# First MLP weight in 14 column-pair places, refilled with resident units one by one; row transfers of the third group issued from GpSimd

## The chip, the core and the metric

The kernel runs on one core of one Trainium2 chip. The core has five engines that work side by side, each with a queue of its own that it takes in order: TensorE (PE; its weight loads are listed apart as PEld), VectorE (DVE), ScalarE (ACT), GpSimd (POOL) and SyncE (SP). SP here does nothing but issue DMA transfers; ACT and POOL issue some as well. All transfers share the core's 16 DMA engines. The metric is device time in microseconds from one execution of the whole program, lower being better; the median of three runs stands for a kernel.

## The reference: what is computed

Two branches are added to the input x (2048 rows of 1024, bfloat16), both of them fed with the normalised rows xn.

```python
xn = _layernorm(x, axis=-1)
return x + _A_ref(xn, mem0, Wq, Wk, Wv, Wo, seg_len) + _B_ref(xn, w1, b1, w2, b2)

# A: a recurrence over 64 segments of 32 rows, 32 heads of 128, 8 memory rows
for s in range(n_seg):
    h = jnp.concatenate([mem, xs], axis=1)                # 40 rows
    q, k, v = h @ Wq, h @ Wk, h @ Wv                      # each 1024 x 4096
    p = _softmax(jnp.where(mask, q k^T * scale, -1e9))
    o = (p v) @ Wo                                        # 4096 x 1024
    mem = o[:, :M, :].copy()
    outs.append(o[:, M:, :])

# B: an MLP
h = _gelu(jnp.einsum('bsd,df->bsf', x, w1) + b1)          # w1 1024 x 3584
return jnp.einsum('bsf,fd->bsd', h, w2) + b2              # w2 3584 x 1024
```

The lines of A are shortened into matrix products. Because a segment's memory is the output of the segment before it, the 64 segments must be done one after another. The four attention weights hold 33.5 MB together[...].

## The kernel before, in words

**The MLP stage.** The rows are handled in four groups (tg 0 to 3) of four tiles of 128 rows. For each group, xn transposed lies in two places (xn0 and xn1 for even groups, xn2 and xn3 for odd ones). The first matrix product (L506) makes 28 column blocks of 128, each of them eight matmuls over the depth of 1024 (kt), then GELU on ACT and DVE writes to gT0 to gT6. The second product (L555, in the last group L591) reads gT and the second weight in 14 places w2_0 to w2_13. Its results are written to a DRAM array R_n (keep_R) and from there copied, in pieces of 8 or 32 rows, to two DRAM arrays hr_d and hrL_d in the order in which the recurrence will want them (turn_R, L425 to L454). The input rows of a group lie in pairs in xt0 to xt3; the last group's in xt2 and xt3.

**The first weight.** It lies in 16 places w1_0 to w1_15, one for each kt and half of the columns, of 128 partitions x 1792 columns. Each column block reads eight of these places, so none is free before its half is done, and load_w1 fills the first half in two column parts.

**The places.** All these names are places of one size (128 x 2048 bfloat16, 0.524 MB). A *unit* is a piece of an attention weight of that size: 16 each for K, Q and V, 16 for O (two heads of Wo). Of the 64 units, 46 are *resident*: they are fetched once, into places which the MLP has left, and stay. The other 18 are *streamed*: fetched for every segment anew, into six ring places, in the order of use. RING and RES_PLACES (L196 to L201) say which place gets which. start_stream (L240 to L256) fills a ring place with the next streamed unit; most streamed units are read from contiguous copies in DRAM (Wc_K, Wc_Q, Wc_V, Wc_O) that the kernel makes at the end of the first group. Two streamed units are held in PSUM banks and copied from there (L240); one of them is brought in through half_home and d_oL. fetch_resident fills places with resident units, and what has no place left is fetched *late*, during segment step 0 (late_units, fetch_late), one unit for each streamed unit that is done.

**The change of stages.** At the start of the last group SP issues the rows for step 0 (load_x_rows, load_left_rows) and refills xt0 and xt1. After the first product of that group it starts the six ring places, loads half_home and the other w1 places; during the second product it refills w2 and gT places as they fall free; after it, xt2 and xt3, which must wait until keep_R has written their contents to R_n.

**The recurrence.** Each of the 64 steps runs K, Q, V (two halves of eight units each, products L705 of four 32-row column tiles) and O (16 units, L902). Between them come transposes, scores, column sums (L834, L840), the exponentials (ACT L845, L848), weights (DVE L855, L859) and values (L874, L880). Step 0 makes, for all six halves, a second product with the rows left over from the 24 main ones (hrL); in the others one or two halves do. After each unit, unit_done refills its ring place, then takes one entry of late_units, then one or two of `small`, a list of small transfers that POOL issues.

**The order.** There is no scheduler: each engine's queue holds the instructions in the order of the program text, and SP's queue is where all weight transfers stand. An SP instruction whose place isn't free holds up all behind it.

Of the kernel before, what the change touches and what calls it, by code (L numbers as in the profile page):

```python
# [17 lines left out]
P = 128  # L18
# [5 lines left out]
F = 3584  # L24
# [3 lines left out]
KT = DM // P  # L28
FC = F // P
# [57 lines left out]
def kernel(  # L87
# [63 lines left out]
    def slab(place):  # L151
        if place in low:
            return low[place]
        return slabs.tile([P, 2048], BF16, name="u", tag=place)
# [38 lines left out]

    RING = [f"xn{k}" for k in range(4)] + [f"w1_{k}" for k in range(16)]  # L196
    RES_PLACES = list(low) + ["xt0", "xt1"] + RING[STREAM_BUFS:]
    RING = RING[:STREAM_BUFS]
    for k in range(7):
        RES_PLACES += [f"w2_{2 * k}", f"w2_{2 * k + 1}", f"gT{k}"]  # L200
    RES_PLACES += ["xt2", "xt3"]  # L201
    UNIT_AT = dict(zip(RES_PLACES, RESIDENT))
    res_tiles = {}


# [17 lines left out]
    def fetch_resident(*places):  # L223
        for place in places:
            unit = UNIT_AT[place]
            res_tiles[unit] = slab(place)[:, :]
            fetch(res_tiles[unit], unit)
# [14 lines left out]
    def start_stream(slot):  # L242
        if not starts:
            return
        n = starts.popleft()
        unit, t = streams[n], slab(slot)
        if unit in kept_in:
            for c0, bank in kept_in[unit]:
                copy_bits(t[:, c0:c0 + 1024].bitcast(U32), bank.bitcast(U32))
        elif unit == PART:  # L250
            nc.sync.dma_start(out=t[:, PART_COLS:], in_=copies[unit])
        elif unit in copies:
            nc.sync.dma_start(out=t[:, :], in_=copies[unit])
        else:
            fetch(t[:, :], unit)
        stream_tiles[n], slot_of[n] = t, slot  # L256
# [8 lines left out]
    def load_left_rows(g, eng=nc.sync):  # L265
        hr = hrp.tile([P, 256], BF16, name="hrL")
        eng.dma_start(out=hr[:, :], in_=hrL_d[g, :, 0:256])
        nxt["hL"] = hr.rearrange("p (k t) -> p k t", k=KT)
# [27 lines left out]
    with tc.tile_pool(name="ma", bufs=2) as ma, tc.tile_pool(name="mps", bufs=6, space=PSUM) as mps:  # L296
# [17 lines left out]
        nc.vector.memset(o_sb[:, 0:8, :], 0.0)  # L314
        w1_sb, w2_sb = [], []

        def load_w1(half):
            for kt in range(KT):
                w1_sb.append(slab(f"w1_{8 * half + kt}")[:, 0:F // 2])
            for c in (0, 1) if half == 0 else (None,):  # L320
                for kt in range(KT):
                    cs = slice(0, F // 2) if c is None else slice(F // 4 * c, F // 4 * c + F // 4)
                    nc.sync.dma_start(
                        out=w1_sb[8 * half + kt][:, cs], in_=w1_v[:, kt, F // 2 * half:F // 2 * (half + 1)][:, cs]
                    )
                if c == 0:
                    nc.sync.dma_start(out=b1rows[:, :], in_=B_b1.rearrange("(fc p) -> fc p", p=P))

        b1rows = ma.tile([FC, P], BF16, name="b1rows", bufs=1)
        load_w1(0)  # L330
        masks_out()
        for j in range(4):
            nc.sync.dma_start(
# [2 lines left out]
            )  # L336
        b2row = ma.tile([1, DM], BF16, name="b2row", bufs=1)
        nc.sync.dma_start(out=b2row[:, :], in_=B_b2.rearrange("(o d) -> o d", o=1))
        load_w1(1)
        for i in range(14):  # L340
            t = slab(f"w2_{i}")[:, :].rearrange("p (c d) -> p c d", d=DM)
            nc.sync.dma_start(out=t, in_=w2_v[:, 2 * i:2 * i + 2, :])
# [79 lines left out]

            return seg % GRP == 1 or seg == NSEG - 1

        def turn_R(ttg, small=None):  # L425

            for i in range(4):
                seg = 4 * ttg + i  # L430
                rows = R_n[seg * SEG:(seg + 1) * SEG, :].rearrange("t (j c) -> t j c", j=4)
                og, slot = divmod(seg + 2, GRP)
                both = [
                    t[:, 256:512].rearrange("(h r) c -> r h c", h=2)
                    for t in (hr_d[min(4 * og + 1, NSEG - 1) + 1, :, :], hrL_d[og, :, :])
                ]
                halves = [rows.rearrange("t (h w) c -> t w h c", w=2)[:, w, :, :] for w in range(2)]
                if with_left(seg):
                    m0 = main_row(slot)
                    pairs = [(both[w][m0:m0 + SEG, :, :], halves[w]) for w in range(2)]  # L440
                else:
                    pairs = [(hr_d[seg + 1, :, 256:512].rearrange("(j t) c -> t j c", j=4), rows)]
                rows_at = [NL * slot]
                if seg < 2:
                    rows_at.append(NL * (slot ^ 2))
                elif seg >= NSEG - 2:
                    rows_at.append(main_row(1) + SEG + NL * slot)
                for r0 in rows_at:
                    pairs += [(both[w][r0:r0 + NL, :, :], halves[w][NX:SEG, :, :]) for w in range(2)]
                for o, r in pairs:  # L450
                    if small is None:
                        nc.sync.dma_start(out=o, in_=r)
                    else:
                        small.append(lambda o=o, r=r: nc.gpsimd.dma_start(out=o, in_=r))  # L454

# [32 lines left out]
        for tg in range(4):  # L488
            last = tg == 3
            if last:  # L490

                load_x_rows(0)
                load_left_rows(0)
                fetch_resident("xt0", "xt1")
            gts = [slab(f"gT{i}")[:, :].rearrange("p (c t) -> p c t", c=4) for i in range(7)]

            def gelu_tail(fb, u, xb):
                sg = ma.tile([P, 512], BF16, name="g_sg")
                nc.scalar.activation(out=sg[:, :], in_=u[:, :], func=ACT.Sigmoid, scale=GELU_C)
                nc.vector.tensor_tensor(out=gts[fb // 4][:, fb % 4, :], in0=sg[:, :], in1=xb[:, :], op=ALU.mult)  # L500

            pend = None
            for fb in range(FC):
                ps = mps.tile([P, 512], F32, name="ps")
                for kt in range(KT):
                    nc.tensor.matmul(  # L506
                        ps[:, :].rearrange("p (s t) -> p s t", t=SEG),
                        lhsT=w1_sb[fb // 14 * 8 + kt][:, (fb % 14) * P:(fb % 14 + 1) * P],
                        rhs=xnT[kt // 4][:, :, kt % 4, :],
                        start=(kt == 0),  # L510
                        stop=(kt == KT - 1),
                    )
                xb = ma.tile([P, 512], BF16, name="g_xb", bufs=3)
                nc.scalar.activation(  # L514
                    out=xb[:, :], in_=ps[:, :], func=ACT.Identity, bias=b1col[:, fb:fb + 1], scale=1.0
                )
                u = ma.tile([P, 512], BF16, name="g_u")
                nc.vector.tensor_tensor(out=u[:, :], in0=xb[:, :], in1=xb[:, :], op=ALU.mult)
                nc.vector.tensor_scalar(
                    out=u[:, :], in0=u[:, :], scalar1=0.044715, scalar2=1.0, op0=ALU.mult, op1=ALU.add  # L520
                )
                nc.vector.tensor_tensor(out=u[:, :], in0=u[:, :], in1=xb[:, :], op=ALU.mult)  # L522
                if pend is not None:
                    gelu_tail(*pend)
                pend = (fb, u, xb)
            gelu_tail(*pend)

            if tg == 0:
# [6 lines left out]
            if not last:  # L535
# [3 lines left out]
                if tg == 0:  # L539
                    for unit, c in copies.items():  # L540
                        fetch(c, unit)
                    fetch_resident(*low)
                for t in range(4):
                    ln_stats(4 * tg + 4 + t, xtoks[4 * tg + 4 + t])
                ln_sqrt(4 * tg + 4, 4 * tg + 8)
# [20 lines left out]
                    keep_R(ttg, rsb)  # L566
                keep_xT(tg + 1, xnT)
                for t in range(4):
                    turn_R(4 * tg + t)
            else:  # L570


                for slot in RING:
                    start_stream(slot)
                h = 4 * IN_BANKS[1] + 2 * IN_BANKS[2]
                nc.sync.dma_start(out=half_home[:, :], in_=Wo_v[:, h, :])
                fetch_resident(*(place for place in RES_PLACES if place.startswith("w1_")))
                put_mem(o_sb, nxt["hT"], mps.tile([P, 512], F32, name="ps"))
                nc.sync.dma_start(out=d_oL[:, :], in_=Wo_v[:, h + 1, :])
                pss = [mps.tile([P, 512], F32, name="ps") for _ in range(6)]  # L580
# [24 lines left out]
                    cp(out=xtoks[4 * tg + n // 2][:, cs], in_=pss[n][:, :])  # L605
                for t in range(4):
                    keep_R(4 * tg + t, xtoks[4 * tg + t])
                fetch_resident("xt2", "xt3")

# [3 lines left out]
    with tc.tile_pool(name="late", bufs=1) as late, \  # L615
# [42 lines left out]
        def fetch_late(unit):  # L658
            t = late.tile([P, 2048], BF16, name="W_" + "_".join(map(str, unit)))[:, :]
            res_tiles[unit] = t  # L660
            fetch(t, unit)

        late_units = deque(RESIDENT[len(RES_PLACES):])

        def unit_done(unit):

            if IS_STREAMED[unit]:
                start_stream(slot_of.pop(used - 1))
                if late_units:
                    fetch_late(late_units.popleft())  # L670
                for _ in range(2 if len(small) > 8 else 1):
                    if small:
                        small.popleft()()
# [7 lines left out]
        for s in range(NSEG):  # L681
            g, i4 = divmod(s, GRP)
            first, final = s == 0, s + 1 == NSEG
            if 1 <= s <= 4:
                turn_R(NT - 5 + s, small)

# [401 lines left out]
```

The softmax here doesn't subtract the row's maximum and nothing guards it: scores larger than these inputs give would overflow.

## Time and profile before

| | |
|---|---|
| runs of the kernel before | 1868.1, 1876.3, 1877.6 us; median 1876.3 us |
| the profiled execution | span 1866.2 us, from its first to its last instruction; the page gives no other time for it, so what lies around the span is known only as the 1.9 to 11.4 us by which the three runs are longer |
| PE busy | 1726.3 us (93%) |
| DVE, ACT, POOL busy | 904.3 us (48%), 650.4 us (35%), 257.7 us (14%) |
| moved by DMA | 613.13 MB, mean 329 GB/s |
| MLP stage | first matmul of L506 at 16.0 us, last of L591 over by about 422 us |
| recurrence | first product at 423.0 us; end of step 0 (ACT's cast of the memory rows, L1004) at 459.2 us, of step 62 at 1838.9 us |

A line of groups in the profile names the source line, the engine, the operation and the tiles (out<-in). A line of waits reads: engine, tile and line, what it waited for, total us, times, longest us. In the timeline, a line has the start, the length, the engine, the line and the transfer, and how many instructions were merged in it; "SPq" is SP's queue, whose issues are not counted as busy. A wait names what came last.

### The profile page before, as it was taken

The page shows a single profiled execution, that of the slowest core. Times are in us where ns is not written, and L with a number is a line of the kernel's source. Part 1 is how long each engine was busy: PE and PEld are TensorE (multiplying, and loading weights), DVE is VectorE, ACT ScalarE, POOL GpSimd, SP SyncE. Part 2 cuts the span into 40 slices and gives each one's busy share as a digit, 9 for nine tenths or more (in the row PEclk, how much of TensorE's full clock was granted, in tenths as well). Part 3 has the DMA queues.
Part 4 walks back from the last instruction along what each step waited for, and adds up shares of the span by engine and source line. Part 5 has one row for each costly group of instructions (what it writes and reads, how often), then busy time and mean ns, then how long its engine had stood idle before and what let it go on. Part 6 is the DMA issues. An engine that isn't in the chain of part 4 may idle for free.

```text
span 1866.2 us, 72871 instructions
## 1 busy us (share of the span) xinstructions
PE 1726.3 (93%) x32208; PEld 938.2 (50%) x32228; DVE 904.3 (48%) x2190; ACT 650.4 (35%) x1384; POOL 257.7 (14%) x511
## 2 busy tenths in 40 slices
PE   7999999998999999988899999999999999999987
PEld 3444444444554555455555555555545454555544
DVE  6657483704444444444444444544444454544443
ACT  6434251602333333333333333333333333333333
POOL 0000000000442111111111211111111111111112
PEclk9999999999999999999999999999999999999999
DMA  9821211399999999999999999999999999999998
GB/s 337 268 57 47 53 45 53 127 364 334 400 382 393 384 397 379 367 364 368 368 377 380 378 392 394 399 390 384 382 384 390 387 381 378 389 402 384 395 372 318
DMA packets 219721, 613.13 MB, mean 329 GB/s; under 512 B 46507, under 2 KB 65755, under 8 KB 219404
## 3 DMA queue, kind: packets, MB, share of 16 engines
q1 hardware_dynamic: 199292, 589.38, 83.1%
q0 software_dynamic: 15872, 16.39, 2.7%
q8 instruction: 252, 4.13, 0.9%
q10 hardware_dynamic: 4240, 2.71, 0.5%
q14 instruction: 65, 0.53, 0.1%
HBM read 594.40 MB, written 29.23 MB: 334 GB/s over the span
## 4 chain that ended last, share of the span: by engine, by line
PE 65%; DMA 21%; DVE 5%; issue 4%; ACT 3%; POOL 1%; DVEq 0%; ACTq 0%; POOLq 0%; SPq 0%
PE acc L705 30%; PE ps L506 10%; DMA u<-Wc_K 10%; PE acc L902 9%; PE ps L555 8%; DMA u<-Wc_O 4%; DMA outL_d<-half_home 2%; DMA u<-Wc_Q 2%; PE ps L591 2%; ACT mixed L848 2%; PE acc L874 2%; DVE b_oL L763 1%; PE mixed L807 1%; DVE pd_main L855 1%; ACT mixed L845 1%
## 5 line engine op out<-in xcount | busy, mean ns | idle before, releaser
L705 PE MATMUL acc<-u,hr_home 128*32 128x512 bf16 x11520 | 784.3, 381 | 34.5 <-issue 11.8
L705 PEld LDWEIGHTS <-hr_home 128*32 128x32 bf16 x12288 | 353.4, 97 | 318.1 <-issue 64.5
L705 PE MATMUL acc<-u,hrL 128*32 128x512 bf16 x2880 | 261.7, 381 | 9.4 <-issue 5.7
L902 PE MATMUL acc<-u,d_oL 128*32 128x256 bf16 (+1 forms) x3552 | 179.7, 291 | 20.5 <-DMA u<-Wc_O 12.4
L506 PE MATMUL ps<-u 128*128 128x512 bf16 x896 | 196.1, 382 | 2.6 <-ACT u L390 2.6
L240 DVE TENSOR_SCALAR u<-kept 128x512 uint32<-128x512 uint32 x254 | 163.5, 686 | 29.2 <-PE acc L902 12.0
L555 PE MATMUL ps<-u 128*128 128x512 bf16 x657 | 146.2, 379 | 0.8
L902 PEld LDWEIGHTS <-b_oL 128*32 128x32 bf16 x3569 | 112.7, 99 | 67.8 <-issue 35.3
L506 PEld LDWEIGHTS <-u 128*128 128x128 bf16 x896 | 88.1, 98 | 109.3 <-issue 4.6
L902 PEld LDWEIGHTS <-d_oL 128*32 128x32 bf16 (+1 forms) x3552 | 104.0, 98 | 73.7 <-issue 32.6
L1052 POOL DMA_DIRECT2D out_dram<-hr_home x188 | 96.6, 515 | 308.8 <-DVE hr_home L1019 296.2
L855 DVE TENSOR_TENSOR pd_main<-half_home,mixed 128x320 bf16<-128x320 bf16 x128 | 62.5, 488 | 157.5 <-ACT mixed L848 155.7
L705 PEld LDWEIGHTS <-hrL 128*32 128x32 bf16 x3072 | 92.0, 96 | 61.6 <-issue 24.9
L763 DVE STREAM_TRANSPOSE b_oL<-b_oL 128x512 bf16<-128x512 bf16 x128 | 90.7, 708 | 62.5 <-ACT b_oL L749 62.5
L902 PE MATMUL acc<-u,b_oL 128*32 128x256 bf16 (+1 forms) x1618 | 107.0, 292 | 14.9 <-DMA u<-Wc_O 10.5
L902 PE MATMUL acc<-W_O,b_oL 128*32 128x256 bf16 (+1 forms) x1776 | 109.4, 291 | 4.7 <-issue 4.5
L262 POOL DMA_DIRECT2D hr_home<-hr_d x58 | 32.4, 558 | 585.1 <-PE acc L705 566.4
L749 ACT CAST kT<-acc 128x512 bf16<-128x512 f32 x64 | 37.5, 586 | 216.9 <-PE acc L705 216.9
L555 PEld LDWEIGHTS <-u 128*128 128x128 bf16 x672 | 65.3, 98 | 77.4 <-DVE g_u L522 0.4
L749 ACT CAST b_oL<-acc 128x512 bf16<-128x512 f32 x128 | 75.2, 587 | 82.1 <-PE acc L705 81.3
L1004 ACT CAST d_oL<-acc 128x256 bf16<-128x256 f32 (+1 forms) x63 | 26.9, 427 | 209.3 <-PE acc L902 209.3
L514 ACT ACTIVATE g_xb<-ps,b1col 128x512 bf16<-128x512 f32 x112 | 76.8, 686 | 61.0 <-PE ps L506 59.8
(123 smaller groups left out, 1968.3 us busy)
## 6 DMA issues: line engine op xcount, KB each, us to landing
u<-Wc_K SPq DMA_DIRECT2D x320, 512.0 KB
u<-Wc_V SPq DMA_DIRECT2D x256, 512.0 KB
u<-Wc_O SPq DMA_DIRECT2D x256, 512.0 KB
u<-Wc_Q SPq DMA_DIRECT2D x128, 512.0 KB
u<-Wc_O SPq DMA_DIRECT2D x64, 320.0 KB
hr_home<-hr_d POOLq DMA_DIRECT2D x58, 128.0 KB, 5.5
u<-in_B_w_dram SPq DMA_DIRECT2D x14, 512.0 KB
u<-in_A_Wq_dram SPq DMA_DIRECT2D x14, 512.0 KB
```

The lines of the kernel that those rows point to most:

```text
L240: nc.vector.tensor_single_scalar(out=out, in_=in_, scalar=0, op=ALU.bitwise_or)
L506: nc.tensor.matmul(ps[:, :].rearrange("p (s t) -> p s t", t=SEG), lhsT=w1_sb[fb // 14 * 8 + kt][:, (fb % 14) * P:(fb % 14 + 1) * P], rhs=x ...
L514: nc.scalar.activation(out=xb[:, :], in_=ps[:, :], func=ACT.Identity, bias=b1col[:, fb:fb + 1], scale=1.0)
L555: nc.tensor.matmul(ps[:, :], lhsT=gts[fc // 4][:, fc % 4, t * P:(t + 1) * P], rhs=w2_sb[fc // 2][:, fc % 2, cs], start=(fc == 0), stop=(fc ...
L591: nc.tensor.matmul(pss[2 * t + nb][:, :], lhsT=gts[fc // 4][:, fc % 4, t * P:(t + 1) * P], rhs=w2_sb[fc // 2][:, fc % 2, nb * 512:nb * 512 ...
L705: nc.tensor.matmul(o, lhsT=lhs[:, i, :], rhs=m, start=(i == seq[0]), stop=(i == seq[-1]), tile_position=(0, 32 * j),)
L749: cp(out=out, in_=ps.rearrange("p (h e) -> p h e", e=32))
L763: nc.vector.transpose(out=home, in_=home)
L848: nc.scalar.activation(out=mixed[:, 160 * b:160 * b + 160], in_=mixed[:, 0:160], func=ACT.Exp, scale=-1.0, bias=off[:, b:b + 1],)
L855: nc.vector.tensor_tensor(out=pdA.rearrange("p c b q -> p b c q"), in0=prA[:, None, :, :].to_broadcast([P, 2, 4, 40]), in1=dd, op=ALU.mult,)
L902: nc.tensor.matmul(acc[r:r + n // 8, c:c + wide], lhsT=lhs[:, 4 * (i % 4) + 2 * u + k, :], rhs=w_t[:, c0 + c:c0 + c + wide], start=(unit = ...
L1052: nc.gpsimd.dma_start(out=out_flat[rows, 256 * j:256 * j + 256], in_=res[32 * j:32 * j + NX, :])
```

## The change

The first weight is now cut by columns: 14 places w1_0 to w1_13, each with two column blocks (256 columns) at the full depth of 1024, so each fills its place (128 x 8 x 256). One transfer fills one place, in runs of 512 bytes, and a column block reads one place only.

The two places saved are called spare0 and spare1. They are filled with resident units at the end of the first group, together with the three low places.

In the last group, a place of the first weight is refilled as soon as its two column blocks are done: w1_0 and w1_1, now ring places, by start_stream, the other twelve by fetch_resident. The ring is now xn0, xn1, w1_0, w1_1, xn2, xn3. half_home, xn0 and xn1 are filled at the start of that group, xn2 and xn3 after its first product.

xt2 and xt3 get the last two resident units, and these are fetched in step 0, as the last two entries of late_units, behind the four late units.

turn_R takes the issuing engine as an argument: for the rows of group 2 (issued at that group's end) it is GpSimd instead of SyncE. The rows of the last group were on GpSimd already.

Line numbers of the changed kernel differ by up to 6 from those of the one before.

```diff
@@ -193,13 +193,16 @@
 
-    RING = [f"xn{k}" for k in range(4)] + [f"w1_{k}" for k in range(16)]
-    RES_PLACES = list(low) + ["xt0", "xt1"] + RING[STREAM_BUFS:]
-    RING = RING[:STREAM_BUFS]
+    NP1 = FC // 2
+    RING = ["xn0", "xn1", "w1_0", "w1_1", "xn2", "xn3"]
+    assert len(RING) == STREAM_BUFS
+    EARLY = list(low) + ["spare0", "spare1"]
+    RES_PLACES = EARLY + ["xt0", "xt1"] + [f"w1_{k}" for k in range(2, NP1)]
     for k in range(7):
         RES_PLACES += [f"w2_{2 * k}", f"w2_{2 * k + 1}", f"gT{k}"]
-    RES_PLACES += ["xt2", "xt3"]
     UNIT_AT = dict(zip(RES_PLACES, RESIDENT))
+    UNIT_AT.update(zip(("xt2", "xt3"), RESIDENT[-2:]))
+    LATE = RESIDENT[len(RES_PLACES):-2]
     res_tiles = {}
 
@@ -314,20 +317,16 @@
         nc.vector.memset(o_sb[:, 0:8, :], 0.0)
         w1_sb, w2_sb = [], []
 
-        def load_w1(half):
-            for kt in range(KT):
-                w1_sb.append(slab(f"w1_{8 * half + kt}")[:, 0:F // 2])
-            for c in (0, 1) if half == 0 else (None,):
-                for kt in range(KT):
-                    cs = slice(0, F // 2) if c is None else slice(F // 4 * c, F // 4 * c + F // 4)
-                    nc.sync.dma_start(
-                        out=w1_sb[8 * half + kt][:, cs], in_=w1_v[:, kt, F // 2 * half:F // 2 * (half + 1)][:, cs]
-                    )
-                if c == 0:
-                    nc.sync.dma_start(out=b1rows[:, :], in_=B_b1.rearrange("(fc p) -> fc p", p=P))
+        def load_w1(pairs):
+            for pair in pairs:
+                t = slab(f"w1_{pair}")[:, :].rearrange("p (k c) -> p k c", k=KT)
+                nc.sync.dma_start(out=t, in_=w1_v[:, :, 256 * pair:256 * pair + 256])
+                w1_sb.append(t)
 
         b1rows = ma.tile([FC, P], BF16, name="b1rows", bufs=1)
-        load_w1(0)
+        load_w1(range(2))
+        nc.sync.dma_start(out=b1rows[:, :], in_=B_b1.rearrange("(fc p) -> fc p", p=P))
+        load_w1(range(2, 6))
         masks_out()
         for j in range(4):
             nc.sync.dma_start(
@@ -336,7 +335,7 @@
             )
         b2row = ma.tile([1, DM], BF16, name="b2row", bufs=1)
         nc.sync.dma_start(out=b2row[:, :], in_=B_b2.rearrange("(o d) -> o d", o=1))
-        load_w1(1)
+        load_w1(range(6, NP1))
         for i in range(14):
             t = slab(f"w2_{i}")[:, :].rearrange("p (c d) -> p c d", d=DM)
             nc.sync.dma_start(out=t, in_=w2_v[:, 2 * i:2 * i + 2, :])
@@ -422,7 +421,7 @@
 
             return seg % GRP == 1 or seg == NSEG - 1
 
-        def turn_R(ttg, small=None):
+        def turn_R(ttg, eng, small=None):
 
@@ -449,7 +448,7 @@
                     pairs += [(both[w][r0:r0 + NL, :, :], halves[w][NX:SEG, :, :]) for w in range(2)]
                 for o, r in pairs:
                     if small is None:
-                        nc.sync.dma_start(out=o, in_=r)
+                        eng.dma_start(out=o, in_=r)
                     else:
                         small.append(lambda o=o, r=r: nc.gpsimd.dma_start(out=o, in_=r))
 
@@ -491,6 +490,10 @@
 
                 load_x_rows(0)
                 load_left_rows(0)
+                h = 4 * IN_BANKS[1] + 2 * IN_BANKS[2]
+                nc.sync.dma_start(out=half_home[:, :], in_=Wo_v[:, h, :])
+                start_stream("xn0")
+                start_stream("xn1")
                 fetch_resident("xt0", "xt1")
             gts = [slab(f"gT{i}")[:, :].rearrange("p (c t) -> p c t", c=4) for i in range(7)]
 
@@ -505,7 +508,7 @@
                 for kt in range(KT):
                     nc.tensor.matmul(
                         ps[:, :].rearrange("p (s t) -> p s t", t=SEG),
-                        lhsT=w1_sb[fb // 14 * 8 + kt][:, (fb % 14) * P:(fb % 14 + 1) * P],
+                        lhsT=w1_sb[fb // 2][:, kt, (fb % 2) * P:(fb % 2 + 1) * P],
                         rhs=xnT[kt // 4][:, :, kt % 4, :],
                         start=(kt == 0),
                         stop=(kt == KT - 1),
@@ -523,6 +526,12 @@
                 if pend is not None:
                     gelu_tail(*pend)
                 pend = (fb, u, xb)
+                if last and fb % 2:
+                    place = f"w1_{fb // 2}"
+                    if place in RING:
+                        start_stream(place)
+                    else:
+                        fetch_resident(place)
             gelu_tail(*pend)
 
             if tg == 0:
@@ -539,7 +548,7 @@
                 if tg == 0:
                     for unit, c in copies.items():
                         fetch(c, unit)
-                    fetch_resident(*low)
+                    fetch_resident(*EARLY)
                 for t in range(4):
                     ln_stats(4 * tg + 4 + t, xtoks[4 * tg + 4 + t])
                 ln_sqrt(4 * tg + 4, 4 * tg + 8)
@@ -566,15 +575,12 @@
                     keep_R(ttg, rsb)
                 keep_xT(tg + 1, xnT)
                 for t in range(4):
-                    turn_R(4 * tg + t)
+                    turn_R(4 * tg + t, nc.gpsimd if tg == 2 else nc.sync)
             else:
 
-                for slot in RING:
-                    start_stream(slot)
-                h = 4 * IN_BANKS[1] + 2 * IN_BANKS[2]
-                nc.sync.dma_start(out=half_home[:, :], in_=Wo_v[:, h, :])
-                fetch_resident(*(place for place in RES_PLACES if place.startswith("w1_")))
+                start_stream("xn2")
+                start_stream("xn3")
                 put_mem(o_sb, nxt["hT"], mps.tile([P, 512], F32, name="ps"))
                 nc.sync.dma_start(out=d_oL[:, :], in_=Wo_v[:, h + 1, :])
                 pss = [mps.tile([P, 512], F32, name="ps") for _ in range(6)]
@@ -605,7 +611,6 @@
                     cp(out=xtoks[4 * tg + n // 2][:, cs], in_=pss[n][:, :])
                 for t in range(4):
                     keep_R(4 * tg + t, xtoks[4 * tg + t])
-                fetch_resident("xt2", "xt3")
 
@@ -660,14 +665,15 @@
             res_tiles[unit] = t
             fetch(t, unit)
 
-        late_units = deque(RESIDENT[len(RES_PLACES):])
+        late_units = deque(lambda unit=unit: fetch_late(unit) for unit in LATE)
+        late_units += [lambda: fetch_resident("xt2"), lambda: fetch_resident("xt3")]
 
         def unit_done(unit):
 
             if IS_STREAMED[unit]:
                 start_stream(slot_of.pop(used - 1))
                 if late_units:
-                    fetch_late(late_units.popleft())
+                    late_units.popleft()()
                 for _ in range(2 if len(small) > 8 else 1):
                     if small:
                         small.popleft()()
@@ -682,7 +688,7 @@
             g, i4 = divmod(s, GRP)
             first, final = s == 0, s + 1 == NSEG
             if 1 <= s <= 4:
-                turn_R(NT - 5 + s, small)
+                turn_R(NT - 5 + s, nc.gpsimd, small)
```

## The prediction

> **What bounds the kernel now.** I read the stretches first, then what TensorE waits for, then SyncE's queue at the one place where the waits are large. The table of stretches has, from the left: length, busy time of PE, PEld, DVE, ACT, POOL, the granted clock, the share in which the DMA engines were busy, and GB/s.
>
> ```profile
> 330.00:360.00 30.00, 30.00 (x140) 13.58 (x139) 25.74 (x71) 20.67 (x35) 0.00 (x0) 1.00 0.18 49
> 360.00:420.00 60.00, 59.53 (x260) 25.45 (x264) 7.05 (x20) 5.46 (x9) 0.00 (x0) 0.94 0.94 356
> 420.00:435.00 15.00, 13.01 (x205) 6.52 (x204) 9.33 (x17) 5.39 (x9) 0.00 (x0) 1.00 0.77 249
> 435.00:455.00 20.00, 14.87 (x320) 8.22 (x323) 6.63 (x17) 5.49 (x14) 0.42 (x1) 0.91 1.02 389
> 460.00:500.00 40.00, 37.31 (x818) 19.85 (x810) 19.86 (x49) 14.35 (x33) 15.39 (x29) 1.00 1.02 399
> ```
>
> The reader is to see three stages. In the last MLP group (316 to 422) PE is full, whether DMA is nearly idle (18%) or nearly full (94%). In segment step 0 (423 to 459) PE has holes: 14.87 of 20 us. After it, PE is full to 93% and DMA to 102%, in every step alike. The waits of PE from 16 to 423 add up to some 4 us in all, none of it for weights; those of 423 to 530 begin with
>
> ```profile
> PE acc L705 <- DMA u<-Wc_Q: 3.0, 1, 3.0
> PE acc L705 <- DMA u<-Wc_K: 1.9, 3, 0.9
> PE acc L705 <- DVE qL_last L749: 1.7, 1, 1.7
> ```
>
> So one wait of 3 us stands out: the second unit of Q's second half, the seventh streamed unit. SyncE's queue (start, length, line, transfer) says why it is late:
>
> ```profile
> 415.43 16.76 SPq L219 DMA_DIRECT2D u<-in_A_Wo_dram  x6
> 432.25 0.46 SPq L914 DMA_DIRECT2D half_home<-in_A_Wo_dram  x1
> 432.75 0.43 SPq L253 DMA_DIRECT2D u<-Wc_Q  x1
> ```
>
> Of those six Wo transfers the last two go to xt2 and xt3. They wait until the results in these places are written to R_n; the queue's waits put 8.4 us on R_n's landings here. Everything behind them on SP waits too. PE released the first stream slot about 423.4 (four matmuls into step 0); its refill was issued at 432.75.
>
> **The change, part by part.**
>
> *The first weight's layout.* It moves 16 + 8 transfers (1,792- and 3,584-byte runs) to 14 transfers of 0.524 MB in 512-byte runs. Here a rule is weighed. The trace first: in its records 2,048 packets of 1,792 B took 77.7 ns each in the first 16 us, that is 16 engines x 1,792 / 77.7 = 369 GB/s; 640 packets of 512 B between 30 and 60 us took 28.9 ns, 283 GB/s. The Trainium skill (DMA: Bandwidth & Descriptors, Specifications) names 512 B as the smallest size at line rate, which would make the layout free. By the rule the 7.34 MB take 20 us, by the rows 26. I take the rows: 6 us later. PE eats a pair in 3.46 us (217.35: 46.79 us for 216 matmuls, times 16), 151 GB/s, so it isn't overtaken. The first matmul at 16.0 waits for ScalarE's copy of the normed rows, and x is still queued first. Issue: 512 KB in 256-byte runs (hr_d from xnT) cost SP 3.35 us for two at 317; half as many runs gives about 1 us each, 14 us against 13.3 for the 24 old ones. The second weight and the next x rows shift by about 6 us: x was issued at 50.96 to 52.87, and the first load of the run landed 2.8 us after its issue (0.81 to 3.60), while VectorE first needs it at 69.66. Some 14 us of cover, so 0. Without it VectorE's statistics would be late, and behind them its additions, which free PSUM.
>
> *The two spare places.* Two units are fetched around 80 instead of after 363: 1.05 MB at 408 GB/s, 2.6 us of DMA, with only R_n's writes, due at 80.8, behind them on SP. 0.
>
> *52 row transfers of group 2 from SP to POOL.* SP issued them from 323.7 to 356.7, 0.62 us each. On POOL they cost 0.55 to 0.6 us each, plus pauses: from 463.8 to 481.3 POOL issued 13 in 17.4 us, 1.34 each. So 52 take between 31 and 70 us; I take the upper, the nearest row, 324 to 394. POOL's next instruction was L267 at 454.6: hidden by 60 us. VectorE is 86% busy in that stretch and PE waits for it from 100% only, so a slowing of it by up to 16% is hidden too; VectorE's transposes took 0.70 us both beside POOL's issues and without them.
>
> *Refills by pairs.* SP now has x and left rows, Wo's half, two streams and xt0/xt1 out by about 327 instead of 366. Then every 3.46 us one place of w1 falls free and SP waits for PE at each (L222 and L253 before). Behind the waiting instruction stand only the next refills and d_oL's load, due at 423.0. 13 places go out by 363: (13 + 4) x 0.524 + 0.26 = 9.2 MB in 40 us, 230 GB/s. Ahead of PE that is worth 0 by itself: PE doesn't wait from 366 to 422, and the backlog it removes had been worked off by then (SP was already waiting for PE, place by place, from 411).
>
> *xt2 and xt3 moved behind the four late units.* This acts. SP's last two refills before step 0 (second weight's last place, gT6) wait for PE's last MLP matmul, 421.9 and 422.4 as now. Then the part of Wo, which waits for VectorE's copy of half_home (423.72 + 0.69 = 424.4), and the first stream at about 424.9 instead of 432.75, 7.85 us sooner. It took 6.03 us to land then: by 431. PE gets there at 435.87. So the wait is gone:
>
> 1. 438.82 - 435.87 = 2.95 us.
> 2. The clock: it stood at one half from 440.07 to 443.48. From 438.82 to the column sums at 442.96 PE made 12 groups of four products, at 0.2155 us each 2.59, and took 4.14: 1.55 us.
> 3. From the sums to 445.69 the chain ScalarE 0.30, 0.38, 0.38, VectorE 0.49, 0.20, 0.61 stays: 0. The masking that the sums need ended at 436.65, before 438.5.
>
> For item 2 a second rule: the Trainium skill (TensorE: Matmul & The Clock Gate, HAM oscillation) warns of idle gaps over about 3.4 us. This gap was 2.95 with small matmuls ahead of it, so by the rule the clock isn't this gap's doing and the sum is 2.95; the record halves it for 3.41 us right after. I take the record: 4.5. For both ends: 2.95 to 4.5.
>
> What is late next? The four late units, the two postponed ones and streams seven to twelve are 12 x 0.524 + 0.2 + R_n's 1.05 = 7.5 MB; at 400 GB/s from 424.9 they land by 443.8, and the last of them that V's second half needs is due about 447. xt2's fetch may block SP till R_n lands (431.8 in this run; perhaps 436 with more traffic beside it); behind it stands then the twelfth stream, due 447. 0, with up to 3 us against it if these slip.
>
> Steps 1 to 63 are the same instructions: 0. They ran 22.25 us each (L1004's cast from 459.2 to 1838.9, 62 intervals), and the first ones were no slower than the rest.
>
> Sum: 2.95 + 1.55 = 4.5 us. On the profiled execution: 1866.2 - 4.5 = 1861.7 us of span. The median shown is 10.1 above that span, and the runs reach from 1868.1 to 1877.6; carried over, 1876.3 - 4.5 = **1871.8 us**. A change of 0.5%, 9.4 us, is about what a measurement of this kernel can tell from none.
>
> **The rivals.**
>
> *DMA carries the head start through.* DMA is busy 99 to 103% of every stretch from 435 on (but 455 to 460). If it and not PE sets the pace, the 7.85 us stay, less 2.6 if the two postponed fetches still cost their time, and the waits for weights and left rows in 457 to 527 (0.9 + 0.6 + 1.2 + 1.0 = 3.7) go as well: 8.9 to 11.5, middle 10.2, 1866.1 us. For it: the full DMA row. Against: those waits occur in later steps just so (27.7 us for Wc_O, Wc_K, Wc_V and Wc_Q from 600 to 1800, 0.5 a step), and DMA fell to 88% at 455 to 460 because six slots were all it may run ahead.
>
> *The wait only moves.* xt2 blocks SP until R_n lands, late streams come late in V or O: gain 0 to 1.5, 1875.6 us. For it: R_n's writes took from 422 to 431.8. Against: eleven streams are out before it, not six.
>
> *POOL becomes the bound: slower.* POOL's queue is in order, and L267 (left rows of the next group) stands behind the 52. If POOL paused so that each took over (454.6 - 4.5 - 324) / 52 = 2.4 us, that load would be late and PE's products with it at 459.7. At 3 us each POOL ends at 480, 30 us late: 1871.8 + 30 = 1902. For it: pauses of 3 to 4 us between POOL's issues at 479 to 513. Against: even there the mean was 1.34.
>
> *The change doesn't do what it says:* early refills move 9 MB and no time. That is in the forecast already.
>
> **How the numbers follow.** Forecast (gain 2.95 to 6) 0.52; DMA carries it 0.34; the wait moves 0.08; POOL 0.06. Own range of the likeliest: 1867 to 1876, from 2.95 to 6 and the runs' spread of half 9.5 us on a median. Faster by over 0.5%: 0.15 of the first (spread alone) and 0.7 of the second, 0.32. Slower: 0.06, the POOL case. Same: the rest, 0.62. The range leaves out most of POOL, and reaches to 11.5 of gain less some spread: 1862 to 1878.
>
> **What would show it.** SP issues the first Wc_Q stream of step 0 near 425, not 432.75. PE's wait for Wc_Q in step 0 is gone, no half clock at 440, and the first L1004 cast (459.2) comes at about 454.7; the intervals after it stay 22.2. DMA shows about 60% from 330 to 420 without a change of PE there, first MLP matmul stays at 16.0. POOL's row transfers of group 2 end before 400. Wrong would be: a PE wait on w1's places before 67, L267 after 452, a wait for xt2's or V's units in step 0, or steps shorter than 22.

## The result and the profile after

The changed kernel took 1873.09 us in the median of 12 runs (1864.4 to 1880.4), the kernel before 1873.04 us in 12 (1868.1 to 1878.4): a ratio of 0.9987 with a 95% interval of 0.9965 to 1.0009. That is 2.4 us less, anything from 6.6 less to 1.7 more, and nothing that can be told from no change by the 0.5% of the prediction. A second comparison, in five rounds, gave 0.9971 (0.9952 to 0.9991). Both together, weighted by their intervals, give 0.9978 (0.9963 to 0.9993), an estimate: 4.1 us less, from 1.4 to 6.8.

The profiled execution of the changed kernel spans 1876.0 us, that of the kernel before 1866.2. These two spans alone would say that the change costs 10 us. They have to be taken apart by stages. First the stretches of the changed kernel, with the columns of the prediction's table:

```profile
330.00:360.00 30.00, 30.00 (x141) 13.62 (x140) 25.76 (x70) 21.16 (x36) 14.40 (x26) 1.00 0.75 257
360.00:420.00 60.00, 58.38 (x283) 25.76 (x290) 9.74 (x24) 6.54 (x12) 7.29 (x13) 1.00 0.67 215
420.00:435.00 15.00, 13.88 (x288) 7.46 (x277) 7.38 (x16) 4.66 (x9) 0.00 (x0) 1.00 1.02 383
435.00:455.00 20.00, 16.86 (x401) 9.81 (x399) 9.21 (x20) 4.95 (x12) 1.94 (x4) 1.00 1.04 399
460.00:500.00 40.00, 35.80 (x789) 19.37 (x785) 17.71 (x44) 13.26 (x31) 14.90 (x28) 1.00 1.02 394
```

The reader is to see the refills moved forward: DMA is busy to 75% from 330 to 360, where it was 18%, and to 67% instead of 94% after it, while PE is full in both: the 58.38 us from 360 to 420, against 59.53, hold the 1.11 us in which PE stood before the first K product, which here comes at 419.00. From 435 to 455 PE has 16.86 us of work instead of 14.87, and the clock stands at 1.00 instead of 0.91. This stretch lies 4 us further on in step 0 than the one before; in the one profile of the changed kernel that starts step 0 as late (e10, 422.97) PE has 17.21 us of work there.

What PE waited for from 423 to 530 begins with

```profile
PE acc L711 <- DVE qL_last L755: 1.9, 1, 1.9
PE mixed L840 <- DVE mixed L243: 1.7, 1, 1.7
PE acc L908 <- DMA u<-Wc_O: 1.3, 4, 0.6
```

The wait of 3.0 us for Wc_Q that led this list is gone. SyncE's queue at the same place:

```profile
411.43 7.37 SPq L222 DMA_DIRECT2D u<-in_A_Wo_dram  x4
420.44 0.34 SPq L920 DMA_DIRECT2D half_home<-in_A_Wo_dram  x1
420.87 0.44 SPq L256 DMA_DIRECT2D u<-Wc_Q  x1
```

Four transfers of Wo stand ahead of Wo's part, not six, and the first stream of step 0 goes out at 420.87, 1.87 us after the first K product (419.00); it was 9.75 us after it (432.75 and 423.00). The first and last casts of the memory rows close step 0 and step 62:

```profile
L1010 ACT CAST d_oL<-acc x63: 372/373/586, 451.0 to 1846.8; 128x256 bf16<-128x256 f32 x47, 128x512 bf16<-128x512 f32 x16
```

So step 0 took 451.0 - 419.0 = 32.0 us, where it was 459.2 - 423.0 = 36.2. Where in step 0 the time went is seen at three places: the first scores, the product behind them, and the first column sum. Before, and after the change:

```profile
435.46 0.20 PE L807 MATMUL mixed<-b_oL,kT 128*32 128x40 bf16 x4
438.82 0.40 PE L705 MATMUL acc<-u,hr_home 128*32 128x512 bf16 x4 [2.95 <-DMA u<-Wc_Q]
442.70 0.39 PE L834 MATMUL mixed<-half_home,small_consts 128*32 128x160 bf16 x4
```

```profile
431.46 0.20 PE L813 MATMUL mixed<-b_oL,kT 128*32 128x40 bf16 x4
431.69 0.41 PE L711 MATMUL acc<-u,hr_home 128*32 128x512 bf16 x4
434.29 0.26 PE L840 MATMUL mixed<-half_home,small_consts 128*32 128x160 bf16 x4
```

From the first scores to the product it took 3.36 us and now 0.23; from there to the sums, work of the same kind, 3.88 and now 2.60. The other 62 steps took 1395.8 us here and 1379.7 before. The experiments ask three things: what of the change made step 0 shorter, why the start of step 0 lies 4 us earlier, and whether the 16 us in the steps are the change's.

All profiled executions of whole kernels, in us (e5, which does less work, is told further down):

| kernel | first K product | step 0 | steps 1 to 62 | ratio to before, interval |
|---|---|---|---|---|
| before, 5 profiles | 423.0, 419.2, 419.5, 419.2, 419.5 | 36.2, 36.5, 36.8, 36.7, 37.0 | 1379.7, 1379.3, 1380.8, 1388.4, 1393.1 | 0.9998 (0.9980 to 1.0015) |
| changed, 4 profiles | 419.0, 419.2, 423.0, 418.9 | 32.0, 32.1, 32.2, 32.2 | 1395.8, 1385.0, 1385.8, 1391.7 | 0.9987 and 0.9971 |
| e1, xt2 and xt3 alone | 423.6 | 34.2 | 1388.0 | 0.9961 (0.9941 to 0.9980) |
| e2, all but xt2 and xt3 | 423.1 | 36.5 | 1385.5 | 1.0001 (0.9979 to 1.0023) |
| e3, rows on SyncE | 422.8 | 32.1 | 1387.9 | 0.9971 (0.9954 to 0.9988) |
| e6, e1 and R_n from GpSimd | 423.2 | 31.7 | 1384.7 | 0.9965 (0.9948 to 0.9982) |

### The profile page after: what moved, and what is told of

It reads as the page before. It is cut to its first block, busy times and chain, and to the rows that moved or that the text cites. A ratio compares the mean times of both kernels' runs of the same rounds, so it can differ in the third digit from the quotient of the medians.

```text
span 1876.0 us, 72878 instructions
## 1 busy us (share of the span) xinstructions
PE 1721.2 (92%) x32208; PEld 935.4 (50%) x32228; DVE 904.7 (48%) x2190; ACT 651.2 (35%) x1384; POOL 286.5 (15%) x563
## 4 chain that ended last, share of the span: by engine, by line
PE 65%; DMA 22%; DVE 5%; issue 4%; ACT 3%; SPq 0%; POOL 0%; DVEq 0%; ACTq 0%; POOLq 0%
PE acc L711 30%; DMA u<-Wc_K 10%; PE acc L908 10%; PE ps L509 9%; PE ps L564 8%; DMA u<-Wc_O 5%; DMA outL_d<-half_home 2%; DMA u<-Wc_V 2%; PE ps L597 2%; DMA u<-Wc_Q 2%; PE acc L880 2%; ACT mixed L854 2%; DVE b_oL L769 1%; PE mixed L813 1%; DVE pd_main L861 1%
## 5 line engine op out<-in xcount | busy, mean ns | idle before, releaser
L243 DVE TENSOR_SCALAR u<-kept 128x512 uint32<-128x512 uint32 x254 | 163.5, 686 | 32.1 <-PE acc L908 11.1
L908 PE MATMUL acc<-u,d_oL 128*32 128x256 bf16 (+1 forms) x3108 | 156.8, 290 | 14.6 <-DMA u<-Wc_O 9.5
L908 PE MATMUL acc<-u,b_oL 128*32 128x256 bf16 (+2 forms) x2062 | 120.2, 289 | 22.1 <-DMA u<-Wc_O 10.6
L854 ACT ACTIVATE mixed<-mixed,small_consts 128x160 f32<-128x160 f32 x256 | 94.2, 368 | 8.4
```

What stands on the lines that cost most here:

```text
L243: nc.vector.tensor_single_scalar(out=out, in_=in_, scalar=0, op=ALU.bitwise_or)
L854: nc.scalar.activation(out=mixed[:, 160 * b:160 * b + 160], in_=mixed[:, 0:160], func=ACT.Exp, scale=-1.0, bias=off[:, b:b + 1],)
L908: nc.tensor.matmul(acc[r:r + n // 8, c:c + wide], lhsT=lhs[:, 4 * (i % 4) + 2 * u + k, :], rhs=w_t[:, c0 + c:c0 + c + wide], start=(unit = ...
```

## The experiments

**One part alone: xt2 and xt3 as late units (e1).** The edit to the kernel before:

```diff
-    RES_PLACES += ["xt2", "xt3"]
     UNIT_AT = dict(zip(RES_PLACES, RESIDENT))
+    UNIT_AT.update(zip(("xt2", "xt3"), RESIDENT[-2:]))
+    LATE = RESIDENT[len(RES_PLACES):-2]
...
-                fetch_resident("xt2", "xt3")
...
-        late_units = deque(RESIDENT[len(RES_PLACES):])
+        late_units = deque(lambda unit=unit: fetch_late(unit) for unit in LATE)
+        late_units += [lambda: fetch_resident("xt2"), lambda: fetch_resident("xt3")]
...
```

> The kernel before, with one part of the change alone: xt2 and xt3 hold the last two resident units and are fetched as the last two of the late units in step 0. First weight, spare places, ring, refills and row transfers stay as before. Theory (this move is the whole gain): the first stream of step 0 is issued within 3 us of the first K product, PE's wait for Wc_Q goes, and step 0 (first K product to ACT's cast of the memory rows, 36.2 us before, 32.0 after) takes 32 us, 31.5 to 33. Rival (the earlier refills are the gain): the weight backlog holds the streams back, and step 0 stays over 35 us. Time: theory -4 us, ratio 0.998; rival 1.000.

The kernel got faster by 0.39% (0.20% to 0.59%), with no part of the new weight layout. But step 0 took 34.2 us, not 32: nearly half the gain was missing. PE's wait for Wc_Q is gone, and in its place stand, later in step 0, four waits for Wc_O, 2.4 us together. SyncE's queue, and below it the queue's own waits from 419 to 436:

```profile
416.04 7.37 SPq L220 DMA_DIRECT2D u<-in_A_Wo_dram  x4
427.16 0.34 SPq L915 DMA_DIRECT2D half_home<-in_A_Wo_dram  x1
427.60 0.44 SPq L254 DMA_DIRECT2D u<-Wc_Q  x1
```

```profile
SPq L915 <- DMA R_n<-u: 3.7, 1, 3.7
```

Wo's part went out 3.55 us after the first K product (423.61), in the changed kernel 1.44 after it. It waited for a write of R_n, with which it shares no data. The list of the built program's instructions tells the tie (the name after "waits" is the semaphore):

```
SP   L915 DMACopy half_home<-in_A_Wo_dram 128x768   [waits DMAHW2, DVE]
ACT  L416 DMACopy R_n<-u 128x1024                   [waits DMAHW2, DVE, Activation]
ACT  L416 DMACopy R_n<-u 128x1024                   [waits DMAHW4, DVE, Activation]
```

In this program the transfers of SyncE and ScalarE share eight completion semaphores in turn, and each waits for the one that used its semaphore last. Here the turn of Wo's part came to the semaphore of R_n's first write. In the changed kernel, with fewer transfers ahead, R_n's four writes have semaphores 7, 0, 2 and 3, and Wo's part has 4.

**The same with R_n's writes from GpSimd (e6).** If that is so, taking R_n's writes off the shared semaphores should bring the missing 2 us, with the old weight layout:

```diff
-            eng = nc.scalar if ttg >= NT - 4 else nc.sync
+            eng = nc.gpsimd if ttg >= NT - 4 else nc.sync
```

> The kernel before with xt2 and xt3 fetched as late units (as in e1_late_only), and the last group's four R_n writes issued from GpSimd's queue instead of ScalarE's. Theory: in e1_late_only step 0 took 34.2 us and not 32 because Wo's part shares one of eight completion semaphores with R_n's first write and so SyncE waited 3.7 us for its landing; with the writes on GpSimd's own semaphores Wo's part goes out within 2 us of the first K product and step 0 takes 31.7 to 32.5 us. Rival (the w1 refills during the first product are worth the other 2 us): step 0 stays at 34 us or more.

```profile
424.67 0.34 SPq L915 DMA_DIRECT2D half_home<-in_A_Wo_dram  x1
425.11 0.54 SPq L254 DMA_DIRECT2D u<-Wc_Q  x1
```

The first K product was at 423.23, Wo's part followed 1.44 us later, and step 0 took 31.7 us. The 2 us were the wait at the shared semaphore. That ScalarE's queue was relieved of four writes as well doesn't explain them, since the changed kernel keeps the writes on ScalarE and has 32.0 us. And the early refills of the first weight's places are worth nothing in step 0: e6 has none of them and is as short there as the changed kernel. Over the whole run e1 and e6 stand at 0.9961 and 0.9965, the changed kernel at 0.9987 and 0.9971: with overlapping intervals, the few lines do no worse than the whole. One thing stays open: e1's runs are 7.3 us shorter, at the least 3.8, and its step 0 only 2.5. The rest can't be found in its one profile, whose other 62 steps took 1388.0 us.

**All but that part (e2).** The changed kernel with xt2 and xt3 fetched behind R_n's writes again:

```diff
+    RES_PLACES += ["xt2", "xt3"]
     UNIT_AT = dict(zip(RES_PLACES, RESIDENT))
-    UNIT_AT.update(zip(("xt2", "xt3"), RESIDENT[-2:]))
-    LATE = RESIDENT[len(RES_PLACES):-2]
+    LATE = RESIDENT[len(RES_PLACES):]
...
                 for t in range(4):
                     keep_R(4 * tg + t, xtoks[4 * tg + t])
+                fetch_resident("xt2", "xt3")
...
-        late_units += [lambda: fetch_resident("xt2"), lambda: fetch_resident("xt3")]
```

> The changed kernel without that one part: xt2 and xt3 are fetched right behind the last group's R_n writes again, ahead of step 0's streams on SyncE. Theory: SyncE stands until R_n has landed, the first stream of step 0 goes out 7 to 10 us after the first K product, and step 0 takes 35 to 36.5 us. Rival (early refills): R_n lands at once on idle DMA engines, and step 0 takes 32 to 33 us. Time against the kernel before: theory 1.000, rival 0.998.

```profile
415.50 16.98 SPq L222 DMA_DIRECT2D u<-in_A_Wo_dram  x6
432.60 0.40 SPq L920 DMA_DIRECT2D half_home<-in_A_Wo_dram  x1
433.05 0.43 SPq L256 DMA_DIRECT2D u<-Wc_Q  x1
```

```profile
PE acc L711 <- DMA u<-Wc_Q: 3.1, 1, 3.1
```

The old picture is back, wait and all: step 0 at 36.5 us, ratio 1.0001. New layout, spare places, refills by pairs and GpSimd's row transfers together are worth nothing that shows.

**Row transfers back on SyncE (e3).**

```diff
-                    turn_R(4 * tg + t, nc.gpsimd if tg == 2 else nc.sync)
+                    turn_R(4 * tg + t, nc.sync)
```

> The changed kernel with the 52 row transfers of group 2 issued by SyncE as before. Theory (they cost nothing on either queue): SyncE's refills of the last group start some 33 us later, near 356, catch up before 411, PE's waits from 16 to 423 stay at 4 us and step 0 at 32 us; time as the changed kernel, within 2 us. Rival (the move to GpSimd frees the refills and so matters): the refills are still running at step 0, PE waits for a resident or streamed unit there and step 0 grows by 1 us or more.

```profile
356.40 0.44 SPq L265 DMA_DIRECT2D hr_home<-hr_d  x1
...
357.89 0.84 SPq L256 DMA_DIRECT2D u<-Wc_K  x2
```

The first refill of the last group went out at 357.89, 33.5 us after the changed kernel's (324.41), and caught up. Step 0 took 32.1 us, the ratio is 0.9971: as the changed kernel with the transfers on GpSimd.

**A quarter of the weight traffic less (e5).**

```diff
-    streams = [unit for _ in range(NSEG) for unit in ORDER if IS_STREAMED[unit]]
+    CUT = {("K", 1, 0), ("Q", 1, 1), ("V", 1, 1), STREAMED_O[0]}
+    streams = [unit for r in range(NSEG) for unit in ORDER if IS_STREAMED[unit] and (r == 0 or unit not in CUT)]
...
+            if s and unit in CUT:
+                return res_tiles[RESIDENT[0] if unit[0] != "O" else RESIDENT[-1]]
             if IS_STREAMED[unit]:
                 used += 1
...
```

> The changed kernel; from step 1 on four of the 18 streamed units are not loaded, and their products read other units' places, so the work of TensorE is the same and a quarter of the weight traffic is gone. Theory (TensorE's gaps put down to issue are instruction packets that wait behind weights in the DMA engines): the idle before PE's matmuls put down to issue, 48 to 60 us from 460 to 1838 so far, falls below 25, and a step falls from 22.3 to 21.5 us or less. Rival (those gaps have nothing to do with the weight traffic): they stay at 48 us or more, and only the waits for weights, 29 to 35 us, go.

A step took 1293.0 / 62 = 20.9 us, in the four profiles of the changed kernel 22.3 to 22.5; the kernel 1771.4 us in the median of two runs, ratio 0.9458 (0.9415 to 0.9500). PE waited for no weight any more. The idle before its matmuls put down to issue, summed over its lines, was 32.9 us from 460 to 1735, where the changed kernel's was 47.2 to 55.1 in its four profiles. The theory's step time came, and for the gaps neither side's number: they fell by about a third and not below 25. So a quarter of the weight traffic is worth 1.5 us of a step of 22.4, but the gaps have another part that stays without it. Some 0.6 of the 1.5 us lies in neither waits nor gaps (an estimate from busy share times step: PE was busy for 20.5 us a step, and for 19.9 in e5); why the same products keep PE busy for less isn't shown.

**The same kernels again (e4, e7 to e11), and the kernel before against itself (e12).** Four profiles in the table are the changed kernel's, five those of the kernel before; these tell what chance does to the stages.

> The changed kernel once more, for the spread of its stages. Theory (chance in the steps hides the gain): step 0 takes 32 us again within 0.5, while steps 1 to 62 differ from the 1395.8 us of the first profile by several us, as the 1379.7 of the kernel before does. Rival (the change slows the steps): steps 1 to 62 take 1390 us or more again.

> The kernel before once more. Theory: step 0 takes 36.2 us within 0.5; steps 1 to 62 differ from the first profile's 1379.7 us by several us, and the start of step 0 differs from 423.0 by up to 4 us with where the half-clock windows fall, so the difference of single spans says nothing of the change. Rival: steps 1 to 62 take 1380 us again within 2, and the changed kernel's steps are slower in truth.

> The kernel before, a third profile. Steps 1 to 62 took 1379.7 and 1379.3 us in the first two, and 1385 to 1396 in four profiles of changed kernels. Theory (chance): this one lies anywhere from 1378 to 1396, most likely above 1383, since both profiled runs so far were 7 to 10 us shorter than the median of 88. Rival (the change slows the steps by 5 us and more): 1380 within 2 again.

> The kernel before, a fourth profile, as the third: theory 1378 to 1396 us for steps 1 to 62, most likely above 1383; rival 1380 within 2.

> The changed kernel, a third profile. Theory: step 0 takes 32.0 us within 0.3, steps 1 to 62 anywhere from 1378 to 1396 us. Rival (the change slows the steps): 1385 us or more, as in its first two.

> The changed kernel, a fourth profile, as the third: theory step 0 at 32.0 us within 0.3, steps 1 to 62 from 1378 to 1396 us; rival 1385 us or more.

> The kernel before, timed against itself in five rounds, since its four profiled executions were some 7 us shorter than the median of its other runs. Theory (those four were drawn short by chance, and the ratios of 0.996 to 0.997 are the change's): the ratio is 1.000 with an interval of about 0.002 to either side. Rival (whatever runs in the second place of a comparison comes out faster): the ratio is 0.998 or less, and the ratios of the others say that much less. Profile: step 0 at 36.5 us within 0.4; steps 1 to 62 from 1378 to 1396 us.

For a while the rival held: three profiles of the kernel before gave 1379.3 to 1380.8 us for the 62 steps, and all of changed kernels 1384.7 and more. The fourth gave 1388.4, the fifth 1393.1. The five of before span 14 us with a mean of 1384.3, the four of the changed kernel 11 us with a mean of 1389.6; the ranges overlap from 1385 to 1393. The kernel before timed against itself gave 0.9998 (0.9980 to 1.0015), so the 0.996 to 0.997 of e1, e3, e4 and e6 don't come from the way of comparing. Its step 0 took 37.0 us, just over the 36.9 that were allowed for. That the steps are wholly unchanged isn't shown: a mean difference of 5.3 us with such spreads leaves room for none and for some. What speaks for none is the runs: against 4.5 us saved in step 0 they show 2.4 and 5.4 us saved in all, with intervals of some 4 us to either side.

## Why the prediction was right

It said 1871.8 us, no difference that can be told, and 4.5 us from step 0; measured were 1873.09 us, no such difference, and in step 0 a mean of 36.65 us in five profiles before against 32.12 in four after: 4.53 us. Two of these agreements are closer than the working earned. The 1871.8 us rest on a median of 1876.3 from three runs; from the 1873.04 of twelve the same sum gives 1868.5. And the 4.53 us hold two errors of about half a microsecond that cancel. By pieces of step 0, means of five and four profiles, taken from the starts of the products shown above, of the first product after the wait for qL_last, and of the cast:

| piece | forecast, us saved | measured |
|---|---|---|
| first scores to the next product: the wait | 2.95 | 3.64 - 0.23 = 3.41 |
| from there to the product behind qL_last: the clock | 1.55 | 7.01 - 5.44 = 1.57 |
| from there to the cast: the rest | 0 | 13.54 - 13.99 = -0.45 |

*The wait (2.95 us).* Right in its cause: e2 brings wait and length back by the fetch of xt2 and xt3 alone, e1 takes the wait away by it alone. The stream was forecast 1.9 us after the first K product and went out 1.87 after it. The size was taken from the profile in which the wait was shortest. PE's wait for Wc_Q in step 0 was 3.0 to 3.5 us in each of the six profiles with the old order of these fetches (five of before, e2), and gone in the eight others.

*The clock (1.55 us).* Right where the row was taken and not the rule, though in the first profile itself it was less: the 4.14 us end at 442.96, and the first column sum stands at 442.70. All six profiles with the wait (five of before, e2) have a half clock of 3.4 us that begins at 435.1 to 440.1; the eight without it have none in step 0. So a gap shorter than the 3.4 us that the Trainium skill names (TensorE: Matmul & The Clock Gate, HAM oscillation) does go with a half clock here: in three of the six it was 3.0 or 3.1 us. The same small matmuls stand at this place in all fourteen profiles; whether they add to it isn't shown.

*The rest of step 0 (0).* Not quite: it cost 0.45 us. xt2's fetch held SyncE up little: it went out at 430.74, and the queue's waits give R_n 1.3 us; no unit of V was late. But the units behind it came late for O: PE waited 0.2 to 0.4 us for Wc_O in step 0 of all four profiles of the changed kernel, and in none of the kernel before. The forecast had named such a slip, with up to 3 us against it.

*The weight's layout (0).* The zero held; both sizes were off, the rule's more. All 14,336 packets of 512 B took 32.2 ns, 255 GB/s, so the weight's share of the DMA engines was 29 us, where the row gave 26 and the rule of line rate from 512 B gave 20. The next x rows were issued at 57.39, as worked out, and VectorE began with them at 68.66, right behind its GELU work (a late load would have shown as a wait there). Eight of the new transfers took SyncE 12.27 us, 1.5 each and not 1.0: mis-sized by the estimate, and hidden.

*The row transfers (0).* Right. GpSimd's queue:

```profile
373.26 0.55 POOL L451 DMA_DIRECT2D hrL_d<-R_n  x1
446.19 0.59 POOL L270 DMA_DIRECT2D hrL<-hrL_d  x1 [72.38 <-PE acc L711]
```

The last of 52 ended at 373.8, 57 us after the first (316.85), 1.1 us each against the 1.34 taken; then GpSimd was idle for 72 us. The slower rival had nothing to stand on.

*The refills (0).* Right, as e6 shows from the other side.

*DMA carries the head start through.* It didn't, though its premise is right in part: e5 shows that weight traffic costs time in the steps. The gain is what PE got in step 0, and the steps after it show none. Where the head start of 7.9 us went isn't shown. That DMA stops once six slots are full, as the prediction argued, doesn't tell it: in the changed kernel's stretches from 420 to 500 DMA is busy at 102 to 104%, with no stop.

What the prediction didn't have is that SyncE's waits depend on how many transfers stand ahead. With e1 for the change, the same working would have been 2 us off in step 0.

## What to carry to other kernels

Ask of each transfer in an in-order queue what it waits for and what stands behind it; here two fetches that waited for a write-back held up the one stream that was needed, and of a change in a dozen places only moving these two shows a gain. Then look at what the transfer behind them waits for: moved alone, they gave little more than half of it in step 0. Nine megabytes moved forward under a full TensorE bought nothing. When a part is expected to save a quarter of a percent, compare the stage it is in, over several profiles: whole spans differed by 15 us from one execution to the next.

## What the runs showed that was not expected

**Completion semaphores are shared in turn.** Eight of them serve both SyncE's and ScalarE's transfers; a transfer waits for its predecessor eight turns back, whatever that is. In e1 it cost SyncE 3.7 us and step 0 from 2.0 (against the changed kernel) to 2.5 (against e6).

**The start of step 0 is one of two times, by chance.** Six of the 14 profiles have the first K product at 422.8 to 423.6, eight at 418.9 to 419.6, with both in the kernel before and in the changed one. The early ones have no half clock at the change of stages. From 370 to 380, the kernel before and the changed one (first profiles; the clock is the third number from the right):

```profile
370.00:380.00 10.00, 10.00 (x35) 3.84 (x35) 0.00 (x0) 0.00 (x0) 0.00 (x0) 0.74 1.03 413
```

```profile
370.00:380.00 10.00, 9.95 (x47) 4.55 (x47) 0.00 (x0) 0.00 (x0) 2.22 (x4) 1.00 0.57 179
```

In all six late ones the clock was half for 6.8 us from 368 or 369, where eight matmuls with a depth of one alternate with full ones; there the first full clock of the run had come at 19.9 to 21.2 us, in the eight others at 18.0 to 19.4. In all six the half clock begins 348.16 us after that first full clock, 102 times 3.413 us. That fits the free-running window of 3.41 us which the Trainium skill describes (TensorE: Matmul & The Clock Gate, Part 1): its place against the kernel's start would then decide whether it catches the thin stretch. No run moved that place on purpose, so this is argued from the times. It is worth 4 us, as much as the change.

**Gaps in TensorE next to instruction packets.** From 460 to 1838 no product and no weight load of PE starts for over 1 us 43 to 56 times in a profile of the kernel before (the distance from one start to the next). In its first profile 31 of 43 such gaps, in the changed kernel's 38 of 50, end within 2 us of the end of a 16 KB packet on the instruction queue, mostly 1.1 to 1.6 us after it; these packets come some 6 us apart, so a third would do so by chance. In e5 it was 27 of 29, up to 1735. In number and length (54 to 76 us together in the five profiles of before) these gaps vary from run to run about as much as the steps do. That late instructions cause them is argued from the times alone.
